# A seventh product split once more: half of a Strassen-type product of a fused attention and feed-forward kernel

## The chip, the cores and the metric

The kernel runs on one core of a Trainium2 chip. The metric is the device time of the program in microseconds, from three runs of the kernel before; one further execution was profiled. TensorE does matrix products, VectorE, ScalarE and POOL (GpSimd) do elementwise work, SP issues most of the transfers. Each engine works through its own instructions in the order in which they were written; engines wait for each other through semaphores.

## The reference

Attention between tokens and a small state in both directions, then a feed-forward layer over all rows:

```python
scores = scale * np.matmul(x, state.transpose(0, 1, 3, 2))   # x (8, 8, 512, 64), state (8, 8, 32, 64)
a = softmax(scores); xread = np.matmul(a, state)
scores2 = scale * np.matmul(state, x.transpose(0, 1, 3, 2))
a2 = softmax(scores2); sread = np.matmul(a2, x)
x = concat([xread, sread]) as (8 * 544, 512) rows
h = x @ w_in                  # 512 -> 2048
out = (h * sigmoid(h)) @ w_out   # 2048 -> 512
```

## The kernel before

The order of the work is written out by hand; the tile layer adds semaphores and buffers, and doesn't reorder. There are eight batches of 512 token rows each, and a last group of 256 state rows (8 batches of 32).

For a batch, `G1` makes the hidden values transposed: for each of 16 feature tiles `ft` two matmuls of 512 columns (L540), with weights `W1` in which the state has already been multiplied into `w_in`, and the normalised attention weights `aT` as moving data. ScalarE's SILU turns the result into `g`, bf16, 128 features by 512 tokens per `ft`. `G1` has two banks of PSUM.

The second product, `g @ w_out`, is done for batches 1 to 7 with a Strassen-Winograd scheme (`class Unit`): tokens, features and output columns are each cut in two, and seven half products take the place of eight. One half product is 256 tokens by 1024 features by 256 columns: 8 feature tiles times 2 token tiles, 16 matmuls of 256 columns (L646, `mm`). They collect in two banks of PSUM: `al` (bank o1; products 1, 6, 5) and `be` (bank o0; products 7, 2, 4, 3, each of which starts o0 anew). Sums of `g` come first: S3 is written over half of `g` (`sums3`), then S2 (`sums2`), S1 = S2 + A11 (`sums1`), S4 (`sums4`). All are VectorE additions. Sums of `w_out`, D1 to D4, are made once (`t_weights`).

One turn of the main loop (L907) handles batch `b`, and prepares batches `n = b + 1` and `m = b + 2`:

- While the G1s of `b` run (`ft` 5 to 15), units of products 1 and 7 are slipped between them (`early`, a quota per step). A unit is one feature tile, two matmuls. S3 is made in two halves at `ft` 5 and 9. At `ft` 9 VectorE also normalises the attention weights of `n` (`norm_t`: a reduction, a reciprocal, a multiplication of which POOL does half; then SP transposes the result into `aT`) and, in some batches, copies x into rows padded for the state's read (`spread_x`). In batch 7 it is the placing of the state rows' input (`place_xm`). Product 1 is copied to `kept[0]`, product 7 to `kept[1]`.
- After `ft` 15: the rest of S2; `group_a`, which is one or two pieces of `W1` of a later batch (two banks each from a ring of four, evicted half by VectorE and half by ScalarE), the transposed scores of `m`, and in batches 1, 4, 6 the state's read `sread`; then products 2, 6, 4. C11 (`block(0, 0)`) is `kept[0]` plus product 2; S1, a spread and S4 stand behind it on VectorE. Product 4 goes into o0 again, so it follows C11's sum.
- Then further pieces of `W1` (`group_b`), product 5, product 3 mixed with the first G1s of `n`, sums, stores, and on POOL the casts of the next x, `cast_x`, whose transpose `transpose_x` SP issues. The scores of the turn that follows read that transpose.

Of the kernel before, what the change touches and what calls it, by code (L numbers as in the profile page):

```python
# [8 lines left out]
FP32 = mybir.dt.float32  # L9
# [9 lines left out]
B = 8  # L19
# [4 lines left out]
DM = 512  # L24
# [18 lines left out]
def kernel(  # L43
# [23 lines left out]
    o1pool = ctx.enter_context(tc.tile_pool(name="o1pool", bufs=1))  # L67
# [21 lines left out]
    w_in_sb = pers.tile([128, 4, DF], BF16)  # L89
    w_out_sb = pers.tile([128, NFT, DM], BF16)  # L90
    wt = pers.tile([128, 4, 8, 256], BF16)
    xs = pers.tile([128, B, 128], BF16)
    xmT = pers.tile([128, 2, 4, NS, 4], BF16)
    x_rows = []
# [501 lines left out]
    def t_weights(which, k0, n, eng=nc.vector):  # L596
        k = ds(k0, n)
        for w in which:
# [6 lines left out]
            else:  # L605
                sub(eng, D4[:, k], B21[:, k], D2[:, k])

    class Unit:
        def __init__(self, b):
            self.b = b  # L610
            self.lo, self.hi = gh[b, 0], None
            self.s1 = spool.tile([128, 8, 256], BF16, tag="s1", name="s1")
            self.s2 = spool.tile([128, 8, 256], BF16, tag="s2", name="s2")
            self.al = psO.tile([128, 2, 256], FP32, tag="o1", name="o")
            self.be = None
            self.o = [
                opool.tile([128, 2, DM], FP32, tag=f"o_sb{i}", name="o_sb") for i in range(2)
            ]
# [39 lines left out]

        def sums2(self, k0, n):
            k = ds(k0, n)  # L660
            sub(nc.vector, self.s2[:, k], self.hi[:, k, 256:512], self.lo[:, k, 256:512])

        def sums1(self):
            for k0 in (0, 4):
                k = ds(k0, 4)
                add(nc.vector, self.s1[:, k], self.s2[:, k], self.lo[:, k, 0:256])

        def sums4(self):
            for k0 in (0, 4):
                k = ds(k0, 4)  # L670
                sub(nc.vector, self.hi[:, k, 0:256], self.hi[:, k, 0:256], self.s2[:, k])

        def block(self, i, c):
            return self.o[i][:, :, ds(256 * c, 256)]
# [4 lines left out]
    o_two = {}  # L679

    def store(b, tt, eng):
        if b < B:
            if tt < 2:
                o_two[tt] = opool.tile([128, 2, DM], FP32, tag=f"o_sb{tt}", name="o_sb")
            o = o_two[tt % 2][:, tt // 2]
        else:
            o = o1pool.tile([128, DM], FP32, tag="o_one", name="o_sb")
        copy(eng, o[:], outs[tt][:])
        if b < B:
            nc.sync.dma_start(out_re[ds(136 * b, 128), tt, :], o)  # L690
        else:
            nc.sync.dma_start(out_sread[ds(512, 32), ds(4 * tt, 4), :], o[:])


    def sread_out_product():
        g = gh[B, 0]
        half = lambda e, t: g[:, ds(8 * e, 8), ds(128 * t, 128)]
        a11, a21, a12, a22 = half(0, 0), half(0, 1), half(1, 0), half(1, 1)
        t8 = lambda nm: spool.tile([128, 8, 128], BF16, tag=nm, name=nm)
        s1, s2 = t8("s1"), t8("s2")  # L700
        u1, u3 = (spool.tile([128, 256], FP32, tag=nm, name=nm) for nm in ("u1", "u3"))
        o = [o1pool.tile([128, DM], FP32, tag=f"o_s{i}", name="o_s") for i in range(2)]
        al = psO.tile([128, 256], FP32, tag="o1", name="o")

        def product(left, right, to=None, first=True, c=0, n=256):
            if to is None:
                to = bank([128, 256], FP32, "o_s")
            for k in range(8):
                nc.tensor.matmul(  # L709
                    to[:, 0:n],  # L710
                    left[:, k],
                    right[:, k, ds(c, n)],
                    start=(first and k == 0),
                    stop=(k == 7),
                    skip_group_check=True,
                )
            return to

        def out(t, c, n, queue):
            queue.dma_start(  # L720
                out_sread[ds(512, 32), ds(4 * t, 4), ds(c, n)], o[t][:, ds(c, n)]
            )

        lo, hi = ds(0, 256), ds(256, 256)
        s3 = a21
        product(a11, B11, al)
        for k0, n in ((0, 6), (6, 2)):
            k = ds(k0, n)
# [6 lines left out]
        copy(nc.scalar, u1[:], al[:])  # L735
        p4 = product(a22, D4)
        add(nc.vector, u1[:], u1[:], o[1][:, hi])
        sub(nc.vector, s2[:], a12, s2[:])
        add(nc.vector, o[1][:, lo], u1[:], p4[:])
        product(s1, D1, al, False)  # L740
        copy(nc.scalar, u3[:], al[:])
        add(nc.vector, o[1][:, hi], o[1][:, hi], u3[:])
# [164 lines left out]
    for b in range(1, B):  # L907
# [1 line left out]
        m = n + 1  # L909
        u = Unit(b)  # L910
        lead = 3 if b == 1 else LEADS
        last = 6 if b < 3 else 8
        todo = [(1, k) for k in range(last)] + [(7, k) for k in range(8)]
        todo += [(1, k) for k in range(last, 8)]
        n_todo = len(todo)

        def unit():
            p, k = todo.pop(0)
            u.mm(p, k)
            if (p, k) == (1, 7):  # L920
                copy(nc.vector, u.kept[0][:], u.al[:])
            if (p, k) == (7, 7):
                copy(nc.vector, u.kept[1][:], u.be[:])

        def early(j):
            while (
                todo
                and todo[0][1] + (0 if todo[0][0] == 1 else 2) <= j - 2
                and (n_todo - len(todo)) * (NFT - lead) < 16 * (j + 1 - lead)
            ):  # L930
                unit()

        for j in range(lead, NFT):
            upto(NFT * b + j + 1)
            if j == 8:
                u.hi = gh[b, 1]
            if j == max(lead, 5):
                if b == 1:
                    t_weights((3,), 4, 4)
                    transpose_x(3)  # L940
                u.sums3(0, 4)
                if 1 < b and m + 1 < B:
                    fetch_x(m + 1)
                if b == 2:
                    for v in range(2):
                        evict_state(v, (nc.vector, nc.gpsimd)[v], 4, 4)
            if j == 9:
                u.sums3(4, 4)
                if b == 1:
                    for v in range(2):  # L950
                        evict_state(v, (nc.vector, nc.gpsimd)[v], 2, 2)
                    t_weights((2, 4), 4, 4, nc.gpsimd)
                elif n < B:
                    norm_t(n)
                    if b in SREAD_AT:
                        spread_x(n)
                else:
                    for half in range(2):
                        place_xm(half, nc.vector)
            early(j)  # L960
            if j == 13:
                u.sums2(0, 4)
# [49 lines left out]
        def units(p, leads={}):  # L1012
            nonlocal step
            for k in range(8):
                u.mm(p, k)
                if n == B and (p != 6 or k > 5):
                    upto(NFT * B + 2 + (step + 1) * (NFT - 2) // 26)
                    step += 1
                    if (p, k) == (3, 1):
                        sread_diff()  # L1020
# [6 lines left out]
        if b == 1:  # L1027
# [5 lines left out]
            fetch_x(m + 1)  # L1033
            exps_t(m)
            out_a()
        else:
# [64 lines left out]
```

## Time and profile before

| | |
|---|---|
| median of 3 runs | 203.32 us (202.95 to 205.41) |
| profiled execution | 202.72 us |
| its span, first to last instruction | 200.9 us |
| mean granted TensorE clock | 1.00 |
| matmuls of G1, 128x512 | x252, 72.7 us busy |
| matmuls of half products, 128x256 | x336, x224 and x224; 48.6, 33.0 and 27.4 us busy |
| VectorE's wait of `o_sb` for TensorE | 23.0 us in 12 waits, the longest 5.1 |
| POOL's wait of `o_sb` for ScalarE | 63.5 us in 13 waits |
| transfers | 28.71 MB, mean 143 GB/s |

Times in the profile are in microseconds from the start of the span; in a timeline row the first number is the start, the second the time from the first start to the last end of the merged instructions, `xN` how many they are. Matmuls are pipelined, so that a row's end lies beyond the start of the next one. `out<-in` names what is written and read. A kernel line can be that of a helper: L162 is any copy on VectorE or POOL, L591 and L594 are subtractions and additions, L646 is any matmul of a half product. By ft 15 of each batch the main loop has reached, in the profiled execution: batch 3 at 90.14 us, batch 4 at 111.13, batch 5 at 133.01, batch 6 at 153.12, batch 7 at 174.20.

### The profile page before, as it was taken

To read this page: it belongs to the slowest core of one execution; us is meant where nothing else is said; L and a number is where in the kernel's file an instruction comes from. 1 tells how busy PE (TensorE), PEld (TensorE's weight loads), DVE (VectorE), ACT (ScalarE), POOL (GpSimd) and SP (SyncE) were. 2 spreads that over 40 slices of the span, in tenths; PEclk is the share of its full clock that TensorE was granted. 3 is DMA by queue.
4 is the path that set the end of the run, shared out by engine and by line. 5 is a ranking of instruction groups with operands and counts; after the bars stand their busy time and mean duration, and the time that the engine had idled before them with its cause. 6 is when DMAs were issued, how large, how long until landed. Compare 5 with 4: busy or idle time off the path is not lost.

```text
span 200.9 us, 4650 instructions
## 1 busy us (share of the span) xinstructions
PE 194.4 (97%) x1912; PEld 130.5 (65%) x1912; DVE 139.3 (69%) x244; ACT 138.3 (69%) x245; POOL 72.3 (36%) x89
## 2 busy tenths in 40 slices
PE   7799999999999999999999999999999999999992
PEld 2444435467766676667766676668666876688881
DVE  2852756989997899388938974779369955872072
ACT  2885657889767887778787957888588167724530
POOL 8674333795535602730373034323202230002200
PEclk9999999999999999999999999999999999999999
DMA  5999999993056995594239912943142005000232
GB/s 193 197 206 207 256 253 353 240 233 86 5 162 181 245 267 111 209 279 90 52 151 200 230 32 55 256 102 30 37 197 55 13 3 209 0 3 0 84 128 104
DMA packets 40821, 28.71 MB, mean 143 GB/s; under 512 B 27360, under 2 KB 37472, under 8 KB 40800
## 3 DMA queue, kind: packets, MB, share of 16 engines
q1 hardware_dynamic: 34592, 20.52, 39.8%
q0 software_dynamic: 5920, 7.64, 18.3%
q8 instruction: 15, 0.25, 0.5%
q10 hardware_dynamic: 288, 0.26, 0.4%
q14 instruction: 6, 0.05, 0.1%
HBM read 17.43 MB, written 8.91 MB: 131 GB/s over the span
## 4 chain that ended last, share of the span: by engine, by line
PE 93%; DMA 4%; DVE 0%; POOL 0%; ACT 0%; issue 0%; POOLq 0%
PE o L646 43%; PE h L540 27%; PE ps_w L473 5%; DMA w_in_sb<-in_moe_w_in_dram 4%; PE h L558 4%; PE o L577 3%; PE o_a L577 3%; PE o_s L709 2%; PE o L709 1%; PE ps_sr L420 1%; PE ps_scT L336 1%; PE ps_busy L168 1%; PE h L522 1%; PE ps_xt L257 1%; PE ps_at L402 1%; PE ps_sc L310 0%
## 5 line engine op out<-in xcount | busy, mean ns | idle before, releaser
L568 ACT ACTIVATE g<-h 128x512 bf16<-128x512 f32 (+1 forms) x142 | 79.9, 573 | 34.5 <-PE h L540 23.7
L646 PEld LDWEIGHTS <-g 128*128 128x128 bf16 x560 | 54.2, 98 | 29.2 <-issue 0.5
L540 PE MATMUL h<-aT,W 128*128 128x512 bf16 x252 | 72.7, 379 | 0.2 <-ACT W L160 0.2
L646 PE MATMUL o<-w_out_sb,g 128*128 128x256 bf16 x336 | 48.6, 273 | 0.0
L646 PE MATMUL o<-wt,g 128*128 128x256 bf16 x224 | 33.0, 273 | 0.0
L594 POOL TENSOR_TENSOR o_sb<-o_sb,kept 128x512 f32<-128x512 f32 x7 | 11.0, 1568 | 54.8 <-ACT o_sb L160 39.6
L540 PEld LDWEIGHTS <-W 128*128 128x128 bf16 x252 | 24.4, 98 | 8.7 <-issue 0.9
L646 PE MATMUL o<-wt,s 128*128 128x256 bf16 x224 | 27.4, 273 | 0.0
L594 DVE TENSOR_TENSOR o_sb<-o_sb,o 128x512 f32<-128x512 f32 x14 | 9.6, 683 | 23.9 <-PE o L646 20.5
L162 DVE CAST W<-ps_w 128x512 bf16<-128x512 f32 (+1 forms) x35 | 21.8, 666 | 6.1 <-PE ps_w L473 5.9
L646 PEld LDWEIGHTS <-s 128*128 128x128 bf16 x224 | 21.5, 98 | 4.4 <-issue 2.0
L160 ACT ACTIVATE W<-ps_w 128x512 bf16<-128x512 f32 (+1 forms) x31 | 16.4, 583 | 5.3 <-PE ps_w L473 5.2
L591 DVE TENSOR_TENSOR g<-g 128x1024 bf16<-128x1024 bf16 x15 | 11.6, 775 | 9.1 <-ACT g L568 9.0
L162 POOL CAST x_nat<-x_f 128x512 bf16<-128x512 f32 x24 | 15.8, 700 | 5.4 <-issue 3.9
L594 POOL TENSOR_TENSOR o_sb<-kept,o_sb 128x512 f32<-128x512 f32 x7 | 8.9, 1268 | 23.9 <-ACT o_sb L160 23.9
L160 ACT ACTIVATE o_sb<-o 128x512 f32<-128x512 f32 x15 | 8.9, 595 | 9.8 <-issue 6.6
L591 DVE TENSOR_TENSOR g<-g,s 128x1024 bf16<-128x1024 bf16 x14 | 13.7, 1019 | 0.0
L366 POOL TENSOR_TENSOR an<-e,rcn 128x512 bf16<-128x512 bf16 x5 | 7.7, 1540 | 16.1 <-DVE rcn L364 15.6
L162 DVE COPY kept<-o 128x512 f32<-128x512 f32 x14 | 9.6, 686 | 4.2 <-PE o L646 4.1
L591 DVE TENSOR_TENSOR s<-g 128x512 bf16<-128x512 bf16 (+3 forms) x23 | 12.0, 550 | 0.1
L577 PEld LDWEIGHTS <-g 128*128 128x128 bf16 x64 | 5.8, 98 | 7.0 <-issue 0.8
L473 PE MATMUL ps_w<-w_in_sb,stT 64*32 64x512 bf16 (+1 forms) x264 | 10.2, 375 | 0.1
(106 smaller groups left out, 214.7 us busy)
## 6 DMA issues: line engine op xcount, KB each, us to landing
out_dram<-o_sb SPq DMA_DIRECT2D x14, 512.0 KB, 2.7
x_f<-in_x_dram SPq DMA_DIRECT2D x6, 512.0 KB, 4.8
x_f<-in_x_dram POOLq DMA_DIRECT2D x2, 1024.0 KB, 11.4
x_f<-in_x_dram SPq DMA_DIRECT2D x2, 1024.0 KB, 6.5
w_out_sb<-in_moe_w_out_dram POOLq DMA_DIRECT2D x6, 256.0 KB, 11.3
w_in_sb<-in_moe_w_in_dram POOLq DMA_DIRECT2D x3, 512.0 KB, 10.5
x_f<-in_x_dram POOLq DMA_DIRECT2D x2, 512.0 KB, 14.5
out_dram<-o_sb SPq DMA_DIRECT2D x4, 256.0 KB, 5.5
```

The source lines that it names most:

```text
L160: nc.scalar.activation(dst, src, func=COPY, bias=0.0)
L162: eng.tensor_copy(dst, src)
L366: eng.tensor_tensor(a[:, hg], e2[b][:, hg], rc[:, hg].to_broadcast([128, 4, 4, NS]), op=MULT)
L473: nc.tensor.matmul(pss[f, hg][ds(32 * s, 32), 0:n], stT[ds(r, 64), b, h // 2, s % 2, :], w_in_sb[ds(r, 64), h // 2, ds(f, n)], start=True, ...
L540: nc.tensor.matmul(h_ps[k][:], W1[b][:, hg, ds(128 * ft, 128)], aT[b][:, hg, :, :], start=(hg == 0), stop=(hg == 1), skip_group_check=True,)
L558: nc.tensor.matmul(ps[:, 0:256], w_in_sb[:, kt, ds(128 * ft, 128)], xmT[:, :, kt].rearrange("p t n b -> p t (n b)"), start=(kt == 0), stop ...
L568: nc.scalar.activation(gt[k], ps[:, 0:n], func=SILU, bias=0.0)
L577: nc.tensor.matmul(outs[tt][:], gt[b * NFT + ft][:, ds(128 * tt, 128)], w_out_sb[:, ft, :], start=(ft == 0), stop=(ft == NFT - 1), skip_gr ...
L591: eng.tensor_tensor(dst, a, c, op=SUB)
L594: eng.tensor_tensor(dst, a, c, op=ADD)
L646: nc.tensor.matmul(to[:, t, :], left[:, ds(128 * t, 128)], right[:, k, :], start=first and t == 0, stop=(k == 7), skip_group_check=True,)
L709: nc.tensor.matmul(to[:, 0:n], left[:, k], right[:, k, ds(c, n)], start=(first and k == 0), stop=(k == 7), skip_group_check=True,)
```

## The change

For batches 3 to 7 product 7, S3 times D3, is itself cut in two three ways and done with seven inner products of 4 matmuls of 128 columns. Inner sums of S3 (`inner_sums`) are made on VectorE at `ft` 5 and 9, and inner sums of D3 (`inner_weights`) once in batch 1. Inner products 1, 6 and 5 collect in a bank of the ring (`chain`), 2, 3, 4 and 7 in quarters of o0; VectorE puts the four quarters of `kept[1]` together after the fifth, which is the last to run. The quota of `early` spreads 15 units over one step less. `norm_t` moves from `ft` 9 of batch `n - 1` to the end of the turn before, behind product 3. `sums1` moves ahead of product 2 and C11. Spreads of x move behind S4, two of them in batch 2. Half of `place_xm` moves to POOL, and before product 2 of batch 7 there is one more G1 of the state rows. Some tiles of the tail share buffers of other tiles.

```diff
+    wt2 = pers.tile([128, 4, 4, 128], BF16)
...
+    def quarters(a):
+        return {
+            (e, c): a[:, ds(4 * e, 4), ds(128 * c, 128)] for e in range(2) for c in range(2)
+        }
+
+    def inner_weights(which, eng):
+        d = [wt2[:, i] for i in range(4)]
+        y = quarters(D3)
+        a, c = {
+            0: (y[0, 1], y[0, 0]),
+            1: (y[1, 1], d[0]),
+            2: (y[1, 1], y[0, 1]),
+            3: (y[1, 0], d[1]),
+        }[which]
+        sub(eng, d[which], a, c)
+
+    INNER = (3, 4, 5, 6, 7)
...
+        def inner_sums(self, which):
+            x = quarters(self.lo[:, :, ds(256, 256)])
+            if self.inner is None:
+                self.inner = spool.tile([128, 4, 4, 128], BF16, tag="s1", name="inner")
+            t = [self.inner[:, i] for i in range(4)]
+            for i in which:
+                if i == 1:
+                    add(nc.vector, t[0], x[0, 1], x[1, 1])
+                elif i == 2:
+                    sub(nc.vector, t[1], t[0], x[0, 0])
+                elif i == 3:
+                    sub(nc.vector, t[2], x[0, 0], x[0, 1])
+                else:
+                    sub(nc.vector, t[3], x[1, 0], t[1])
+
+        def inner_mm(self, i):
+            x, y = quarters(self.lo[:, :, ds(256, 256)]), quarters(D3)
+            t, d = self.inner, wt2
+            if self.chain is None:
+                self.chain = bank([128, 128], FP32, "o_ch")
+                self.be = psO.tile([128, 2, 256], FP32, tag="o0", name="o")
+            q = self.be.rearrange("p t (c n) -> p (t c) n", c=2)
+            ch = self.chain[:]
+            left, right, to, where = {
+                1: lambda: (x[0, 0], y[0, 0], ch, 1),
+                2: lambda: (x[1, 0], y[1, 0], q[:, 0], 0),
+                3: lambda: (t[:, 3], y[1, 1], q[:, 2], 0),
+                4: lambda: (x[1, 1], d[:, 3], q[:, 1], 0),
+                5: lambda: (t[:, 0], d[:, 0], ch, 1),
+                6: lambda: (t[:, 1], d[:, 1], ch, 1),
+                7: lambda: (t[:, 2], d[:, 2], q[:, 3], 0),
+            }[i]()
+            for k in range(4):
+                nc.tensor.matmul(to, left[:, k], right[:, k],
...
+            kept = self.kept[1]
+            if i == 1:
+                copy(nc.vector, kept[:, 0, 0:128], ch)
+            elif i == 6:
+                copy(nc.vector, kept[:, 1, 0:128], ch)
+            elif i == 5:
+                first = kept[:, :, 0:128]
+                u3 = spool.tile([128, 1, 128], FP32, tag="inner_u3", name="inner_u3")
+                copy(nc.vector, u3[:, 0], ch)
+                add(nc.vector, kept[:, :, 128:256], q[:, 2:4], u3.to_broadcast([128, 2, 128]))
+                add(nc.vector, first, first, q[:, 0:2])
+                add(nc.vector, kept[:, 1, 0:128], kept[:, 1, 0:128], q[:, 3])
...
-        last = 6 if b < 3 else 8
-        todo = [(1, k) for k in range(last)] + [(7, k) for k in range(8)]
-        todo += [(1, k) for k in range(last, 8)]
+        inner = b in INNER
+        if inner:
+            todo = [(1, k - 8, k + 2) for k in range(7)] + [(7, 1, 9), (1, -1, 9)]
+            todo += [(7, 2, 10), (7, 4, 10), (7, 7, 11), (7, 6, 12), (7, 3, 12), (7, 5, 13)]
+        else:
+            last = 6
+            todo = [(1, k - 8, k + 2) for k in range(last)]
+            todo += [(7, k - 8, k + 4) for k in range(8)]
+            todo += [(1, k - 8, k + 2) for k in range(last, 8)]
...
             while (
                 todo
-                and todo[0][1] + (0 if todo[0][0] == 1 else 2) <= j - 2
-                and (n_todo - len(todo)) * (NFT - lead) < 16 * (j + 1 - lead)
+                and todo[0][2] <= j
+                and (n_todo - len(todo)) * (NFT - lead - bool(inner)) < n_todo * (j + 1 - lead)
             ):
                 unit()
...
                 u.sums3(0, 4)
+                if inner:
+                    u.inner_sums((3,))
...
                 u.sums3(4, 4)
+                if inner:
+                    u.inner_sums((1, 2, 4))
...
-                elif n < B:
-                    norm_t(n)
-                    if b in SREAD_AT:
-                        spread_x(n)
-                else:
+                elif b == 2:
+                    norm_t(3)
+                elif n == B:
                     for half in range(2):
-                        place_xm(half, nc.vector)
+                        place_xm(half, (nc.vector, nc.gpsimd)[half])
...
         if 2 < b < B - 1:
             out_a()
+        if b > 1:
+            u.sums1()
         if n == B:
-            upto(NFT * B + 2)
+            upto(NFT * B + 3)
...
-        else:
-            u.sums1()
-            if n < B and b not in SREAD_AT:
-                spread_x(n)
...
         units(4)
         u.sums4()
+        if 1 < b < B - 2:
+            for i in {2: (3, 4)}.get(b, (b + 2,)):
+                spread_x(i)
         add(nc.vector, u.block(1, 0), u.block(1, 0), u.be[:])
...
         if b == 1:
             group_b()
+            for i in range(4):
+                inner_weights(i, (nc.vector, nc.gpsimd)[i % 2])
         units(3, {1: 2, 3: 3, 5: 4, 7: 5})
+        if 1 < b and m < B:
+            norm_t(m)
         add(nc.vector, u.block(0, 1), u.block(0, 1), u.be[:])
```

More of the change, by code (lines that the diff above doesn't have):

```diff
@@ L66 @@
     opool = ctx.enter_context(tc.tile_pool(name="opool", bufs=1))
-    o1pool = ctx.enter_context(tc.tile_pool(name="o1pool", bufs=1))
     spool = ctx.enter_context(tc.tile_pool(name="spool", bufs=1))
@@ L611, in __init__ @@
             self.lo, self.hi = gh[b, 0], None
-            self.s1 = spool.tile([128, 8, 256], BF16, tag="s1", name="s1")
-            self.s2 = spool.tile([128, 8, 256], BF16, tag="s2", name="s2")
+            self.s1 = self.s2 = None
             self.al = psO.tile([128, 2, 256], FP32, tag="o1", name="o")
             self.be = None
+            self.chain = None
+            self.inner = None
+            self.begun = set()
             self.o = [
@@ L660, in sums2 @@
             k = ds(k0, n)
+            if k0 == 0:
+                self.s2 = spool.tile([128, 8, 256], BF16, tag="s2", name="s2")
             sub(nc.vector, self.s2[:, k], self.hi[:, k, 256:512], self.lo[:, k, 256:512])
         def sums1(self):
+            self.s1 = spool.tile([128, 8, 256], BF16, tag="s1", name="s1")
             for k0 in (0, 4):
@@ new lines, in inner_mm @@
+        def inner_mm(self, i):
[16 more added lines that the diff above has]
+            for k in range(4):
+                nc.tensor.matmul(
+                    to,
+                    left[:, k],
+                    right[:, k],
+                    start=where not in self.begun,
+                    stop=(k == 3),
+                    skip_group_check=True,
+                )
+                self.begun.add(where)
+            kept = self.kept[1]
[7 more added lines that the diff above has]
+                copy(nc.vector, u3[:, 0], ch)
+                add(
+                    nc.vector,
+                    kept[:, :, 128:256],
+                    q[:, 2:4],
+                    u3.to_broadcast([128, 2, 128]),
+                )
+                add(nc.vector, first, first, q[:, 0:2])
+                add(nc.vector, kept[:, 1, 0:128], kept[:, 1, 0:128], q[:, 3])
@@ L681, in store @@
     def store(b, tt, eng):
[L682 to L685, printed above, removed]
-        else:
-            o = o1pool.tile([128, DM], FP32, tag="o_one", name="o_sb")
+        if tt < 2:
+            o_two[tt] = opool.tile([128, 2, DM], FP32, tag=f"o_sb{tt}", name="o_sb")
+        o = o_two[tt % 2][:, tt // 2]
         copy(eng, o[:], outs[tt][:])
-        if b < B:
-            nc.sync.dma_start(out_re[ds(136 * b, 128), tt, :], o)
-        else:
-            nc.sync.dma_start(out_sread[ds(512, 32), ds(4 * tt, 4), :], o[:])
+        nc.sync.dma_start(out_re[ds(136 * b, 128), tt, :], o)
     def sread_out_product():
@@ L700, in sread_out_product @@
         s1, s2 = t8("s1"), t8("s2")
-        u1, u3 = (spool.tile([128, 256], FP32, tag=nm, name=nm) for nm in ("u1", "u3"))
-        o = [o1pool.tile([128, DM], FP32, tag=f"o_s{i}", name="o_s") for i in range(2)]
+        both_u = xpool.tile([128, 4, 256], FP32, tag="x_nat", name="u")
+        u1, u3 = both_u[:, 0], both_u[:, 1]
+        o = [spool.tile([128, DM], FP32, tag=f"kept{i}", name="o_s") for i in range(2)]
         al = psO.tile([128, 256], FP32, tag="o1", name="o")
@@ L734, in sread_out_product @@
         add(nc.vector, s1[:], s2[:], a11)
-        copy(nc.scalar, u1[:], al[:])
+        copy(nc.scalar, u1, al[:])
         p4 = product(a22, D4)
-        add(nc.vector, u1[:], u1[:], o[1][:, hi])
+        add(nc.vector, u1, u1, o[1][:, hi])
         sub(nc.vector, s2[:], a12, s2[:])
-        add(nc.vector, o[1][:, lo], u1[:], p4[:])
+        add(nc.vector, o[1][:, lo], u1, p4[:])
         product(s1, D1, al, False)
-        copy(nc.scalar, u3[:], al[:])
-        add(nc.vector, o[1][:, hi], o[1][:, hi], u3[:])
+        copy(nc.scalar, u3, al[:])
+        add(nc.vector, o[1][:, hi], o[1][:, hi], u3)
         out(1, 0, 512, nc.sync)
@@ L911 @@
         lead = 3 if b == 1 else LEADS
-        last = 6 if b < 3 else 8
-        todo = [(1, k) for k in range(last)] + [(7, k) for k in range(8)]
-        todo += [(1, k) for k in range(last, 8)]
+        inner = b in INNER
[7 more added lines that the diff above has]
+            todo += [(1, k - 8, k + 2) for k in range(last, 8)]
         n_todo = len(todo)
         def unit():
[L918 to L923, printed above, removed]
+            p, k, _ = todo.pop(0)
+            if k > 0:
+                u.inner_mm(k)
+                return
+            u.mm(p, k + 8)
+            if k == -1:
+                copy(
+                    nc.vector,
+                    u.kept[int(p == 7)][:],
+                    (u.al if p == 1 else u.be)[:],
+                )
         def early(j):
@@ L952 @@
                     t_weights((2, 4), 4, 4, nc.gpsimd)
-                elif n < B:
-                    norm_t(n)
-                    if b in SREAD_AT:
-                        spread_x(n)
-                else:
+                elif b == 2:
+                    norm_t(3)
+                elif n == B:
                     for half in range(2):
-                        place_xm(half, nc.vector)
+                        place_xm(half, (nc.vector, nc.gpsimd)[half])
             early(j)
@@ L1016, in units @@
                 if n == B and (p != 6 or k > 5):
-                    upto(NFT * B + 2 + (step + 1) * (NFT - 2) // 26)
+                    upto(NFT * B + 3 + (step + 1) * (NFT - 3) // 26)
                     step += 1
@@ L1035 @@
             out_a()
-        else:
-            u.sums1()
-            if n < B and b not in SREAD_AT:
-                spread_x(n)
         if m < B:
```

## The prediction

> **What bounds the kernel now.** I read the page's busy times first, then the chain that ended last, then TensorE's waits, and then VectorE and TensorE side by side where a batch's seventh product ends.
>
> ```profile
> PE 194.4 (97%) x1912; PEld 130.5 (65%) x1912; DVE 139.3 (69%) x244; ACT 138.3 (69%) x245; POOL 72.3 (36%) x89
> ...
> PEclk9999999999999999999999999999999999999999
> ...
> PE 93%; DMA 4%; DVE 0%; POOL 0%; ACT 0%; issue 0%; POOLq 0%
> ```
>
> TensorE carries the chain (93%) at the full clock, and none of its waits after the first 10 us is longer than 0.2 us. A column removed from it is therefore worth its time, and a wait added to it costs its time: nothing later has idle time that would absorb it. What matters is whether VectorE, 69% busy on average, is late anywhere. In batch 6 (ft 15's G1 starts at 153.12) VectorE answers
>
> ```profile
> 153.97 0.69 DVE L162 COPY kept<-o 128x512 f32<-128x512 f32 x1
> 154.58 0.75 DVE L591 TENSOR_TENSOR s<-g 128x512 bf16<-128x512 bf16 x2
> 155.25 0.68 DVE L162 CAST W<-ps_w 128x512 bf16<-128x512 f32 x1
> 155.85 0.74 DVE L438 RECIPROCAL rc<-ps_sr 32x4 f32<-32x4 f32 x4
> 156.63 0.42 DVE L441 TENSOR_TENSOR xm<-ps_sr,rc 128x256 bf16<-128x256 f32 x1
> 156.97 0.68 DVE L162 CAST W<-ps_w 128x512 bf16<-128x512 f32 x1
> 157.57 0.68 DVE L594 TENSOR_TENSOR o_sb<-kept,o 128x512 f32<-128x512 f32 x1
> 158.16 1.28 DVE L594 TENSOR_TENSOR s<-s,g 128x1024 bf16<-128x1024 bf16 x2
> ```
>
> and TensorE
>
> ```profile
> 155.04 1.92 PE L646 MATMUL o<-w_out_sb,g 128*128 128x256 bf16 x16
> 156.80 1.91 PE L646 MATMUL o<-wt,s 128*128 128x256 bf16 x16
> 158.55 0.71 PE L646 MATMUL o<-wt,g 128*128 128x256 bf16 x5
> ```
>
> VectorE has no gap from 153.97 to the end of S1. The C11 sum (157.57, done 158.25) reads bank o0, which product 4 overwrites at 158.55: 0.2 us of room. So in this stretch VectorE is as late as TensorE allows.
>
> **What the matmuls give.** The half product goes from 16 matmuls of 256 columns to 7 x 4 = 28 of 128. The tail has both kinds, back to back:
>
> ```profile
> 194.25 1.04 PE L709 MATMUL o<-wt,s 128*128 128x256 bf16 x8
> ...
> 196.00 1.06 PE L709 MATMUL o_s<-w_out_sb,s 128*128 128x128 bf16 x16
> ```
>
> The last of a group takes 0.27 or 0.22, so (1.04 - 0.27)/7 = 0.11 us each for 256 columns (0.109 over sixteen) and (1.06 - 0.22)/15 = 0.056 for 128. That makes 16 x 0.109 = 1.74 against 28 x 0.056 = 1.57: 0.18 less a batch, 0.9 in five. The upper end for 128 columns is a weight load that hides behind nothing, 98 ns in the page's LDWEIGHTS groups: 28 x 0.098 = 2.74, 1.0 more a batch than now. I take 0.056: it is the same shape, with a new weight for each.
>
> The Trainium skill (TensorE: Matmul & The Clock Gate, Back-to-back issue gap) speaks against the split: it gives some 81 ns for a matmul of 128 columns in a stream of weight loads and matmuls. By that the half product would take 28 x 0.081 = 2.27, half a microsecond more than now, and the sum below would be 3.5 us higher. The row above is such a stream and contradicts it.
>
> **What VectorE gets.** (1) Four inner sums of 128x512 bf16, 0.33 each by the pair at 154.58: one behind the first half of S3, three behind the second. Normalisation and spread left that place (1.21 + 0.35 + 0.69, and 0.69 to 1.54), and TensorE needs the sums only three or four G1s later; without that cover 1.0. Nothing. (2) The last inner product now stands ahead of ft 15's G1, because the quota ends a step earlier. With T the start of that G1, its last matmul ends at T + 0.16 (0.22 - 0.056), and a copy starts 0.04 after that (in batch 3 the matmul ends at 90.95, the copy starts at 90.99). Then a copy of 128x128, two additions of 128x256 and one of 128x128 must free o0. Rows: 0.42 for 128x256 from PSUM, 0.29 for an addition of 128x128; 0.03 between dependent ones, 0.08 overlap otherwise. A copy of 128x128 isn't shown; between 0.2 and 0.42 I take 0.29. Sum 0.29 + 0.03 + 0.42 - 0.08 + 0.42 + 0.03 + 0.29 = 1.40, done T + 1.61. The wait sits on the weight load, so product 2 starts some 0.18 later, T + 1.79. (3) S1, two of 0.60, moves ahead of the C11 sum.
>
> From T, with the s2 halves after the chain (T + 1.53 to 2.20), W casts 0.60 each, and product 4 at 0.08 after C11:
>
> - Batches 3 and 5: product 2 at T + 1.79 (before: 90.14 to 91.76, 1.62). Two casts to 3.40, S1 to 4.61, C11 to 5.30, product 4 at T + 5.38; before 95.26 - 90.14 = 5.12. 0.26 late each.
> - Batch 4: product 2 waits as now for scores that follow ft 15's SILU (T + 2.51). Cast 2.80, reciprocals and product of the s read 4.11, S1 5.32, C11 6.01, product 4 at 6.09 against 6.01. 0.08 late.
> - Batch 6: casts, reciprocals and product as above to 4.52, S1 to 5.73, C11 to 6.42, product 4 at 6.50; before 158.55 - 153.12 = 5.43. 1.07 late.
> - Batch 7: no casts; C11 waits for product 2 anyway, which follows SILUs. Nothing.
>
> Up to T a batch has 8 units of 0.218 and 7 of 0.224 where it had 15 of 0.218: 0.04 later, 0.2 in five. Sum: 0.26 + 0.08 + 0.26 + 1.07 + 0.2 = 1.9 us **longer**; that is the 0.9 gained, less 2.8 of new waits. Without S1's move batch 6 would be 1.07 less, so that move is the largest single term. A POOL operation beside S1 would lengthen it (S4 took 2.36 beside one, 1.28 without): up to 1.1 more; with quicker small evictions 0.4 less a batch.
>
> **What moves.** Normalisation (2.3 on VectorE) comes before the last C21 sum, where VectorE waits for TensorE 2.2 to 2.5 us: hidden. But on POOL its multiplication now stands ahead of the four casts of x, and on SP the aT transpose ahead of the last store, the xT transpose and the x load. In batch 3 the casts started at 102.64; W casts end at 100.8, reduction and reciprocal at 102.4, POOL's 1.54 after its sum at 102.70 ends at 104.25: 1.6 later. The xT transpose, issued at 105.41 with a median of 5.0 to landing, is read at 112.10: 1.7 of room. Three batches (2, 3, 4) have this; at the longest landing, 7.0, each would wait 1.6 to 2. I take 0.1 in all. Spreads behind S4 stand ahead of the sum that frees o0 for product 3: in batch 4 1.4 of room (120.54 to 121.94) against 0.69 to 1.54, in batch 2 two spreads, about 0.7 of room after S1 has filled a wait of 0.39: 0 to 1.0 altogether, I take 0. The weights of the inner product (two operations on VectorE, two on POOL at about 1.1, half of 2.2) fall into idle 1.51 (before 61.50) and 3.90 (before 62.56). POOL takes half of place_xm where it has nothing else. Buffers that share tags are long free. All 0; on the path they would be 1 to 3 us.
>
> The profiled run of before took 202.72 (span 200.9, 1.8 around it): 202.72 + 1.9 + 0.1 = 204.7. The median of the runs is 203.32, 0.6 higher, which would give 205.3. Prediction 205.0.
>
> **Rivals.** *The gain stays* (0.24): VectorE's evictions or S1 come earlier than my rows say, and only the 0.9 is left: 202.72 - 0.9 = 201.8, on the median 202.4. For it: VectorE loses 2 to 4 us per batch ahead of T. Against it: the row at 153.97 waits for TensorE, not for VectorE's own backlog, so nothing done earlier helps. *Late xT* (0.10), on the slower side: the casts that stand behind the normalisation make scores wait in the next batch; it decides once a landing takes over 5.1. Three waits of 1.6 to 2 make 4.8 to 6 on top of 1.9: 209.5 to 210.6. For it: SP's queue gets another transpose ahead of it; against it: 3.7 is the shortest. *Weight loads show* (0.06): at 0.098 a matmul, 5 x 28 x 0.042 = 5.9 more: 210.5. *The change isn't what it says* (0.01): the order of the built program shows 28 for 16 in five batches, so hardly.
>
> **How the numbers follow.** The forecast has 0.59: its own range is 204.0 to 206.3 (product 4 waits 0.7 less in all, or the s sums and spreads meet POOL). Within 2% is about what a measurement of this kernel can tell from no change: 199.3 to 207.4. The gain and the forecast lie inside: 0.24 + 0.59, and 0.03 of mild lateness of xT; slower takes the rest of late xT, weight loads and S1 beside POOL, 0.12; faster 0.02. The range reaches down to most of the rival, 202.0, and up to 207.0, and leaves some 2 in 10 out.
>
> **What would show it.** The 28 small matmuls at about 56 ns each; three small VectorE sums ending 1.6 us after ft 15's G1 starts; product 4 named as waiting for the VectorE sum o_sb<-kept,o, some 1.1 us in batch 6 and 0.1 to 0.3 in 3, 4 and 5; product 2 waiting for the kept sums in 3 and 5; scores without a wait for xT. I am wrong if TensorE has no such waits, or if C11 ends earlier than S1 lets it, or if TensorE waits in batches 2 and 4 for o0 ahead of product 3.

## The result, and the profile after

The changed kernel takes 205.28 us (median of 22 runs, 204.33 to 207.49). The kernel before, run beside it on the same chip, takes 203.41 (22 runs, 202.56 to 205.52). The medians are 1.9 us (0.9%) apart. The ratio, which leaves out one run of after that was in a slower state, is 1.007, with a 95% interval of 1.0044 to 1.0096, or 1.4 us. So the change costs 1.4 to 1.9 us. The profiled execution took 205.22, with a span of 203.4 at a mean granted clock of 0.997; before it was 202.72, with a span of 200.9.

The page of after, at the places shown of before: busy time and share of the span, granted clock by slice, chain that ended last.

```profile
PE 194.8 (96%) x1972; PEld 130.4 (64%) x1972; DVE 154.3 (76%) x287; ACT 137.8 (68%) x245; POOL 80.2 (39%) x95
...
PEclk9999999999999999999999999999999999999998
...
PE 19%; DVE 1%; issue 0%
```

TensorE has 60 matmuls more (12 in each of five batches) and is not less busy; VectorE carries 15 us more. The chain is followed back through the last fifth of the span only (19% and 1%), so it says nothing of the batches; TensorE's waits do. Before, there was one after the first 10 us, and it was 0.2:

```profile
PE h L540 <- ACT W L160: 0.2, 1, 0.2
```

In after two are longer:

```profile
PE o L666 <- DVE o_sb L594: 1.1, 1, 1.1
PE ps_scT L336 <- DMA xT<-x_nat: 0.9, 2, 0.4
```

The first is product 4 of batch 6, the second the transposed scores in batches 4 and 5. Both are new. VectorE in batch 6, where the prediction showed before (start, time from first start to last end; ft 15's G1 starts at T = 154.51):

```profile
154.71 0.29 DVE L162 COPY inner_u<-o_ch 128x128 f32<-128x128 f32 x1
155.03 0.42 DVE L594 TENSOR_TENSOR kept<-o,inner_u 128x256 f32<-128x256 f32 x1
155.37 0.73 DVE L594 TENSOR_TENSOR kept<-kept,o 128x256 f32<-128x256 f32 x2
156.02 0.76 DVE L591 TENSOR_TENSOR s<-g 128x512 bf16<-128x512 bf16 x2
156.69 0.68 DVE L162 CAST W<-ps_w 128x512 bf16<-128x512 f32 x1
157.30 0.74 DVE L438 RECIPROCAL rc<-ps_sr 32x4 f32<-32x4 f32 x4
158.07 0.43 DVE L441 TENSOR_TENSOR xm<-ps_sr,rc 128x256 bf16<-128x256 f32 x1
158.41 0.68 DVE L162 CAST W<-ps_w 128x512 bf16<-128x512 f32 x1
159.01 1.28 DVE L594 TENSOR_TENSOR s<-s,g 128x1024 bf16<-128x1024 bf16 x2
160.21 0.68 DVE L594 TENSOR_TENSOR o_sb<-kept,o 128x512 f32<-128x512 f32 x1
```

and TensorE there, products 2, 6 and 4:

```profile
156.21 1.92 PE L666 MATMUL o<-w_out_sb,g 128*128 128x256 bf16 x16
157.97 1.91 PE L666 MATMUL o<-wt,s 128*128 128x256 bf16 x16
160.94 1.91 PE L666 MATMUL o<-wt,g 128*128 128x256 bf16 x16 [1.07 <-DVE o_sb L594]
```

S1 (159.01) now stands between the W cast and the C11 sum (160.21, done 160.89). Product 4 overwrites the bank that this sum reads, and starts 0.05 after it, at T + 6.44; before it was T + 5.43.

To see where all of the time lies, take T in each batch as the clock and read from the timelines when product 4 starts after it. T2 is the T of batch 2, T3 that of batch 3, and so on; the last column runs from T2 to the end of the span. Differences of these times are free of what happens at the start, where executions of the same code differ by several tenths:

| kernel | b3 | b4 | b5 | b6 | T2 to end |
|---|---|---|---|---|---|
| before | 5.12 | 6.01 | 5.12 | 5.43 | 131.70 |
| after | 5.32 | 6.11 | 5.44 | 6.44 | 133.73 |
| difference | 0.20 | 0.10 | 0.32 | 1.01 | 2.03 |

The four product 4s make 1.63 of the 2.03. From product 4 to the next T is 0.03 to 0.06 longer in each of batches 3 to 6, 0.16 in all; from batch 7's T to the end it is 0.02. From T2 to T3 it is 0.22 longer, 0.18 of it where the scores of batch 2 start later, 0.04 after xT lands. The other 0.45 of the two spans lies ahead of T2, and isn't put down to the change: two of the kernels below whose code is the same up to there (called both and best) have T2 at 69.20 and 70.04.

### The profile page after: what moved, and what is told of

The parts are those of the page before. It is cut to its first block, busy times and chain, and to the rows that moved or that the text cites. A ratio compares the mean times of both kernels' runs of the same rounds, so it can differ in the third digit from the quotient of the medians.

```text
span 203.4 us, 4815 instructions
## 1 busy us (share of the span) xinstructions
PE 194.8 (96%) x1972; PEld 130.4 (64%) x1972; DVE 154.3 (76%) x287; ACT 137.8 (68%) x245; POOL 80.2 (39%) x95
## 5 line engine op out<-in xcount | busy, mean ns | idle before, releaser
L666 PEld LDWEIGHTS <-g 128*128 128x128 bf16 x480 | 46.4, 98 | 24.7 <-issue 1.7
L666 PE MATMUL o<-w_out_sb,g 128*128 128x256 bf16 x336 | 49.3, 273 | 0.2 <-DVE kept L162 0.2
L540 PEld LDWEIGHTS <-W 128*128 128x128 bf16 x252 | 23.4, 98 | 8.2 <-issue 0.9
L666 PE MATMUL o<-wt,g 128*128 128x256 bf16 x144 | 19.3, 273 | 1.1 <-DVE o_sb L594 1.1
L162 POOL CAST x_nat<-x_f 128x512 bf16<-128x512 f32 x24 | 18.5, 809 | 1.5 <-DMA x_f<-in_x_dram 1.5
L591 DVE TENSOR_TENSOR g<-g 128x1024 bf16<-128x1024 bf16 x15 | 12.5, 834 | 3.9 <-ACT g L568 3.8
L591 DVE TENSOR_TENSOR s<-g 128x512 bf16<-128x512 bf16 (+3 forms) x23 | 11.1, 510 | 0.1
L577 PEld LDWEIGHTS <-g 128*128 128x128 bf16 x64 | 5.8, 98 | 7.0 <-issue 0.8
L591 DVE TENSOR_TENSOR g<-g,s 128x1024 bf16<-128x1024 bf16 x14 | 10.2, 772 | 0.0
L577 PE MATMUL o_a<-w_out_sb,g 128*128 128x512 bf16 x32 | 10.0, 379 | 0.0
L594 DVE TENSOR_TENSOR s<-s,g 128x1024 bf16<-128x1024 bf16 x15 | 9.7, 684 | 0.0
```

The lines of the kernel that those rows point to most:

```text
L162: eng.tensor_copy(dst, src)
L540: nc.tensor.matmul(h_ps[k][:], W1[b][:, hg, ds(128 * ft, 128)], aT[b][:, hg, :, :], start=(hg == 0), stop=(hg == 1), skip_group_check=True,)
L577: nc.tensor.matmul(outs[tt][:], gt[b * NFT + ft][:, ds(128 * tt, 128)], w_out_sb[:, ft, :], start=(ft == 0), stop=(ft == NFT - 1), skip_gr ...
L591: eng.tensor_tensor(dst, a, c, op=SUB)
L594: eng.tensor_tensor(dst, a, c, op=ADD)
L666: nc.tensor.matmul(to[:, t, :], left[:, ds(128 * t, 128)], right[:, k, :], start=first and t == 0, stop=(k == 7), skip_group_check=True,)
```

## The experiments

All ten compute the whole of the reference. Times are medians; the ratio is to the kernel before, run on the same chip in the same series, and it is the one to compare where two kernels are of different series.

**S1 back behind product 6 and C11.**

```diff
-        if b > 1:
-            u.sums1()
         if n == B:
             upto(NFT * B + 3)
...
             out_a()
+        else:
+            u.sums1()
```

> S1 goes back behind C11's sum, to its old place after product 6; all else as changed. Theory (S1 ahead of C11 makes product 4 wait in batch 6): the wait of 1.1 there and the 0.16 in batch 3 go, C11 in batch 6 is done before TensorE reaches product 4, and the median is 1.2 to 1.4 lower than the changed kernel, 203.9 to 204.1. Rival (the longer chain of evictions of the seventh product is what makes C11 late, wherever S1 stands): product 4 of batch 6 still waits 0.8 or more, median 204.8 to 205.3.

203.87 us (12 runs), ratio 1.0027 (1.0002 to 1.0052). C11 is first again, S1 after it:

```profile
158.88 0.68 DVE L594 TENSOR_TENSOR o_sb<-kept,o 128x512 f32<-128x512 f32 x1
159.48 1.29 DVE L594 TENSOR_TENSOR s<-s,g 128x1024 bf16<-128x1024 bf16 x2
```

Product 4 of batch 6 starts at T + 5.24, 1.20 sooner: two additions of 0.60. From T2 to the end it is 132.23, 1.50 less than after. The place of S1 is the largest part of the loss. Scores still wait for xT, 0.4 us in one batch.

**S1 behind C11 in batch 6 alone.**

```diff
-        if b > 1:
+        if b > 1 and b != 6:
             u.sums1()
...
+        elif b == 6:
+            u.sums1()
```

> The changed kernel with S1 behind C11 in batch 6 alone. Theory (the wait of batch 6 is the one large cost of S1's place): 1.1 to 1.25 lower than the changed kernel, 204.0 to 204.2; from batch 6's last G1 to batch 7's 21.0 where the changed kernel took 22.15, and the other batches as in the changed kernel. Rival (the waits of the other batches count as much): 204.6 to 205.0.

204.01 us (12 runs), ratio 1.0035 (1.001 to 1.0059). One batch carries most of what S1's place costs: the ratio falls from 1.007 to 1.0035, where moving S1 in all batches gave 1.0027 (the intervals overlap), and from T6 to T7 both kernels take 20.96, where after took 22.15. In batches 3 and 5 S1's place costs 0.16 each: product 4 starts at T + 5.32 in the next run, where xT is in time and S1 ahead of C11, and at T + 5.16 in the run after that, where S1 is behind.

**Casts of x ahead of POOL's half of the normalisation, and the xT transpose ahead of that of aT.**

```diff
         if 1 < b and m < B:
-            norm_t(m)
+            rest = norm_t(m, m + 1 < B)
...
             transpose_x(m + 1)
+            if b > 1:
+                rest()
```

(`rest` is POOL's multiplication and the aT transpose; VectorE's part stays.)

> At the end of a turn POOL's half of the normalisation and the aT transpose go behind the casts of x and the xT transpose; VectorE's part stays. Theory (xT lands late because its casts stand behind the normalisation): the two waits of the transposed scores for xT, 0.44 idle each, go; part returns in their place, because product 2 then waits for the kept sums in batch 5 and product 4 for C11 in batches 4 and 5; median 0.5 to 0.9 below the changed kernel, 204.4 to 204.8. Rival (the transpose is late by SP's other transfers): the waits stay, median 205.3.

205.51 us (6 runs, 204.31 to 207.21), ratio 1.0105 (1.0052 to 1.0158). The gain of 0.5 to 0.9 that was expected didn't come: the time can't be told from that of after. The trace says why a gain is small. No scores wait for xT, but product 4 starts at 5.32, 6.03, 5.32 and 6.44 after T, and in batch 6 still waits for C11:

```profile
162.95 1.25 PE L680 MATMUL o<-wt,g 128*128 128x256 bf16 x10 [1.07 <-DVE o_sb L608]
```

In batches 4 and 5 only 0.08 and 0.12 come back for 0.9 of waiting removed: the scores' second half then waits for ScalarE's last SILU, and product 4 of batch 5 for S1. T2 to end is 133.37, 0.36 less than after, but half of that lies between T2 and T3, which the edit doesn't reach: it starts with the transpose at the end of turn 2, which batch 3 reads. From T3 on it is 0.19. Waits that stand one behind the other don't add.

**Both of these repairs together.** The edits above, S1 in all batches.

> Both edits together. Theory: the split's 0.9 isn't earned even then, because product 2 stands behind the evictions and the last SILU with no unit between: 203.1 to 203.5, about the kernel before. Rival (with these two waits gone nothing hides the shorter TensorE work): 202.4 to 202.7, 0.4% under the kernel before.

203.27 us (12 runs), ratio 0.9986 (0.9965 to 1.0006): back at the kernel before, with the split in it. T2 to end is 132.23, against 131.70 before, and 0.45 of the difference lie between T2 and T3, nearly all of it where the scores of batch 2 wait for xT in this execution. From T3 to the end it is 110.90 against 110.81. So both losses are named, and the question is where the 0.9 us of saved matmul time is.

**The moves without the split.**

```diff
-    INNER = (3, 4, 5, 6, 7)
+    INNER = ()
```

> No batch has its seventh product split (16 matmuls of 256 columns again, one copy to kept[1], no inner sums); every move stays. Theory (the moves lose the time, the split itself gains some): product 4 waits about 1.0 in batch 6 and 0.2 in 3 and 5, xT about 0.4 twice; 205.2 to 205.9. Rival (the split's small operations lose it, the moves are free): 203.2 to 203.6.

204.82 us (11 runs), ratio 1.0072 (1.0041 to 1.0102): by the ratio as slow as with the split. Product 4 starts at 5.26, 6.02, 5.26 and 6.38, so late by 0.14, 0.01, 0.14 and 0.95. The moves alone lose most of the time: T2 to end is 133.06, 1.36 more than before, where the whole change takes 2.03 more. It is somewhat faster than expected, as xT is late in one batch only, by 0.3.

**The repaired moves without the split.** The kernel with both repairs, and `INNER = ()`.

> As 'both', without the split (16 matmuls of 256 columns again, one copy). Theory: the moves without S1's and with the casts ahead cost nothing: 203.2 to 203.6, within 0.1% of 'both', so that the split by itself gives nothing there. Rival (the split in 'both' does give 0.9, and the remaining moves take it): 204.0 to 204.4.

203.52 us (12 runs), ratio 1.0024 (0.9998 to 1.005). The trace has product 4 at 5.12, 6.01, 5.12 and 5.43 as before. From T3 to the end it takes 110.88, against 110.90 with the split: in the two profiled executions the split gives nothing in that form. (The medians are of two series; their ratios to the kernel before, 1.0024 and 0.9986, have intervals that overlap by little, and would leave it some 0.8.) The rows of TensorE behind ft 15 of batch 3 show it, first with the split:

```profile
90.54 0.59 PE L554 MATMUL h<-aT,W 128*128 128x512 bf16 x2
91.07 0.62 PE L487 MATMUL ps_w<-w_in_sb,stT 64*32 64x512 bf16 x16
91.51 0.72 PE L336 MATMUL ps_scT<-xT,stT 64*32 64x512 bf16 x8
92.20 0.61 PE L680 MATMUL o<-w_out_sb,g 128*128 128x256 bf16 x4
```

and without:

```profile
90.68 0.60 PE L554 MATMUL h<-aT,W 128*128 128x512 bf16 x2
91.12 0.38 PE L680 MATMUL o<-w_out_sb,g 128*128 128x256 bf16 x2
91.43 0.63 PE L487 MATMUL ps_w<-w_in_sb,stT 64*32 64x512 bf16 x16
91.87 0.50 PE L336 MATMUL ps_scT<-xT,stT 64*32 64x512 bf16 x8
92.30 0.50 PE L680 MATMUL o<-w_out_sb,g 128*128 128x256 bf16 x3
```

Without the split, a unit of the half products stands behind ft 15 and the scores take 0.50. With it, that unit is ahead of ft 15, and the scores take 0.72: their second half follows ScalarE's SILU of ft 15, the second of the two SILUs (ft 14 and 15) in this row, which ends at 91.77

```profile
90.52 1.25 ACT L582 ACTIVATE g<-h 128x512 bf16<-128x512 f32 x2 [0.28 <-PE h L554]
```

Product 2 starts at T + 1.66 with the split and at T + 1.62 without, though there is a unit less between. What comes off the matmuls before T is lost again behind it.

**Evictions earlier, and one unit left behind ft 15.** Both repairs, and:

```diff
-            elif i == 5:
+            elif i == 3:
                 first = kept[:, :, 0:128]
+                add(nc.vector, first, first, q[:, 0:2])
+                add(nc.vector, kept[:, 1, 0:128], kept[:, 1, 0:128], q[:, 3])
+            elif i == 5:
...
-                add(nc.vector, first, first, q[:, 0:2])
-                add(nc.vector, kept[:, 1, 0:128], kept[:, 1, 0:128], q[:, 3])
...
-            todo = [(1, k - 8, k + 2) for k in range(7)] + [(7, 1, 9), (1, -1, 9)]
-            todo += [(7, 2, 10), (7, 4, 10), (7, 7, 11), (7, 6, 12), (7, 3, 12), (7, 5, 13)]
+            todo = [(1, k - 8, k + 2) for k in range(7)] + [(7, 1, 9)]
+            todo += [(7, 2, 10), (7, 4, 10), (7, 7, 11), (7, 6, 12), (7, 3, 12), (7, 5, 13), (1, -1, 15)]
...
-                and (n_todo - len(todo)) * (NFT - lead - bool(inner)) < n_todo * (j + 1 - lead)
+                and (n_todo - len(todo)) * (NFT - lead) < n_todo * (j + 1 - lead)
...
+            if j == 13 and inner:
+                u.sums2(0, 4)
             early(j)
-            if j == 13:
+            if j == 13 and not inner:
                 u.sums2(0, 4)
```

> The two edits of 'both', and the end of the seventh product rearranged: of its four last VectorE operations the two that need only inner products 1 to 4, 6 and 7 run ahead of inner product 5's copy, S2's first half runs before the step's units, and the last unit of product 1 is left to stand behind ft 15's G1, as a unit did in the kernel before. Theory (what kept the split's gain from showing is the eviction chain and the SILU after the last G1 with no unit between): bank o0 is free 0.9 after ft 15's G1 starts, product 2 starts 1.6 after it as before, and each batch keeps its 0.18: 202.4 to 202.7, ratio 0.995 to 0.997. Rival (128-column matmuls between G1s aren't worth their 56 ns each): 203.1 to 203.5.

202.51 us (12 runs, 201.96 to 203.53) against 203.17 before (29 runs): ratio 0.9968 (0.9944 to 0.9991), 0.3% faster than the kernel before, and faster than after. Behind ft 15 of batch 3, TensorE has its unit again, and the scores take 0.50:

```profile
90.90 0.59 PE L554 MATMUL h<-aT,W 128*128 128x512 bf16 x2
91.33 0.38 PE L680 MATMUL o<-w_out_sb,g 128*128 128x256 bf16 x2
...
92.09 0.50 PE L336 MATMUL ps_scT<-xT,stT 64*32 64x512 bf16 x8
```

Product 4 stands at the places of before, and from T3 to T4 it is 20.81 where before had 20.99: the 0.18 a batch. T2 to end is 131.45, 0.25 less than before. Most of the rest of the gain is lost in three small gaps on the inner products' way (0.17 in batch 5, 0.23 and 0.05 in batch 7) and in one of 0.16 at an early G1 of batch 3. That G1 starts at 80.46, 0.05 after VectorE's cast of its weights, and the cast stands behind the two spreads of batch 2. Against the repaired moves without the split, run in the same series, the split is now worth 1.0 us in the medians and 0.5 in the traces.

**The same without the unit behind ft 15.**

```diff
-            todo = [(1, k - 8, k + 2) for k in range(7)] + [(7, 1, 9)]
-            todo += [(7, 2, 10), (7, 4, 10), (7, 7, 11), (7, 6, 12), (7, 3, 12), (7, 5, 13), (1, -1, 15)]
+            todo = [(1, k - 8, k + 2) for k in range(7)] + [(7, 1, 9), (1, -1, 9)]
+            todo += [(7, 2, 10), (7, 4, 10), (7, 7, 11), (7, 6, 12), (7, 3, 12), (7, 5, 13)]
...
-                and (n_todo - len(todo)) * (NFT - lead) < n_todo * (j + 1 - lead)
+                and (n_todo - len(todo)) * (NFT - lead - bool(inner)) < n_todo * (j + 1 - lead)
```

> As 'best', but product 1's last unit stays where the change put it, so that ft 15's G1 is followed by no unit. Theory: product 2 then waits in batches 3 and 5 for the scores, whose second bank ft 15's SILU frees 1.28 after its G1 starts; 0.1 to 0.3 of the gain is left: 203.0 to 203.3. Rival (the chain of evictions alone held the gain): 202.4 to 202.7, the same as 'best'.

203.96 us (12 runs), ratio 1.004 (1.0019 to 1.0061): worse than expected. The place of one unit decides 1.45 us between this kernel and the one above it in the medians, and 1.03 from T2 to the end. Product 2 starts at T + 1.62 in batches 3 and 5 of both kernels, with the unit before it or not, and from product 4 to the next T it takes 0.22, the time of a unit, longer here. TensorE's waits show a part of it: the scores wait for the last SILU once more, and in batch 7 an inner product waits for the copy that frees its bank:

```profile
PE o_ch L743 <- DVE kept L162: 0.5, 1, 0.5
PE ps_scT L336 <- ACT g L582: 0.2, 1, 0.2
```

So earlier evictions alone don't help: the wait behind ft 15 isn't for them.

**place_xm earlier in batch 7**, on top of the best kernel, to take away its gaps there.

```diff
                     u.inner_sums((3,))
+                if n == B:
+                    for half in range(2):
+                        place_xm(half, (nc.vector, nc.gpsimd)[half])
```

(and taken out at ft 9)

> As 'best', with the state rows' input placed at ft 5 of batch 7 and not at ft 9. Theory (there VectorE's four copies stand ahead of the small evictions and delay inner products 6 and 5 by 0.2 to 0.3): batch 6's last G1 to batch 7's takes 20.8 to 20.9 in place of 21.19, the median 0.2 to 0.4 under 'best': 202.1 to 202.3. Rival (the step is long for another reason): no difference, 202.5.

202.69 us (12 runs), ratio 0.9958 (0.9934 to 0.9982). That can't be told from the best kernel, and T6 to T7 takes 21.13, not 20.8 to 20.9: the rival is nearer. The two gaps ahead of inner products 6 and 5 are gone from the trace, and one of 0.19 is at inner product 2 instead.

**The split alone.** Kernel before, with the split and none of the moves: normalisation and spreads at ft 9, S1 behind C11, place_xm on VectorE.

```diff
-                elif b == 2:
-                    norm_t(3)
-                elif n == B:
+                elif n < B:
+                    norm_t(n)
+                    if b in SREAD_AT:
+                        spread_x(n)
+                else:
...
-        if 1 < b and m < B:
-            norm_t(m)
```

(against after; S1, the spreads and place_xm as before, too)

> The kernel before with the split alone: normalisation and spreads at ft 9, S1 behind C11, all of place_xm on VectorE, two state-row G1s ahead of product 2. Theory (VectorE's queue at ft 9 is full): the copy of inner product 1 stands behind normalisation, and in batches 4 and 6 a spread as well, so that inner product 6 waits about 0.9 in batches 3 and 5, 2.4 in 4 and 6 and 1.5 in batch 7: 209 to 212. Rival (these steps are hidden there as they were before): 202.5 to 203.5.

211.71 us (4 runs, 210.45 to 213.26), ratio 1.0422 (1.0376 to 1.0469). VectorE in batch 4:

```profile
109.35 1.21 DVE L363 TENSOR_REDUCE rs<-e 128x32 f32<-128x1024 bf16 x1
110.60 0.35 DVE L364 RECIPROCAL rcn<-rs 128x32 f32<-128x32 f32 x1
110.99 0.69 DVE L366 TENSOR_TENSOR an<-e,rcn 128x512 bf16<-128x512 bf16 x1
111.60 1.54 DVE L162 COPY x_rows<-x_nat 128x2048 bf16<-128x2048 bf16 x1
113.06 0.28 DVE L162 COPY kept<-o_ch 128x128 f32<-128x128 f32 x1
```

and TensorE, which waits for that copy to use the bank again:

```profile
113.39 0.38 PE L729 MATMUL o_ch<-wt,inner 128*128 128x128 bf16 x4 [2.11 <-DVE kept L162]
...
113.83 0.98 PE L540 MATMUL h<-aT,W 128*128 128x512 bf16 x2
114.61 0.64 PE L729 MATMUL o_ch<-wt,inner 128*128 128x128 bf16 x4
```

There are five such waits, 7.0 us in all. The chain of small evictions stands behind the normalisation (batches 3 to 6) and the spread (4 and 6) on VectorE, and in batch 7 behind the copies of place_xm (1.4). So the moves of those three are what the split needs; S1's move is not, since none of these waits is for it.

## Why the prediction was right, and where not

205.0 was forecast and 205.28 measured, and the forecast's mechanism carries the largest term: S1 in batch 6. That the sum for product 4 comes out to 0.04 (1.67 forecast, 1.63 measured) is in part luck, since in batches 4 and 5 another wait stands where S1's was put. By its steps:

**Matmuls.** 56 ns for 128 columns is right. Four of them and the next instruction are 0.22 apart, here ahead of ft 15 of batch 3 in after:

```profile
90.59 0.39 PE L729 MATMUL o_ch<-wt,inner 128*128 128x128 bf16 x4
90.81 0.38 PE L540 MATMUL h<-aT,W 128*128 128x512 bf16 x1
```

Each has a new weight. The 81 ns of the Trainium skill (TensorE: Matmul & The Clock Gate, Back-to-back issue gap) would be 0.32; the measurement decides. The rival of weight loads that show falls.

**Inner sums hidden.** Right in cost. In size not: they take 0.4 to 0.7 each in batch 3 and not 0.33, but TensorE comes for them later.

**The evictions.** Forecast to end at T + 1.61; in batch 3 of after they end at T + 1.60 (copy 0.29, additions 0.42 and 0.73). Product 2 was put 0.18 after that, at T + 1.79, and starts at T + 1.66, 0.06 after them. It stands behind scores that wait for the last SILU, and loses only 0.04 to the evictions.

**Product 4.** Forecast late by 0.26, 0.08, 0.26 and 1.07 in batches 3 to 6; measured 0.20, 0.10, 0.32 and 1.01. In 3 and 6 the cause is S1 and the evictions, as said. In 4 and 5 it is not: there product 2 is late already (T + 2.60 and T + 1.94 against 2.51 and 1.62), because scores wait for xT, and product 4 follows it at the 3.50 that products 2 and 6 take. In the casts-first run, without that wait, S1 and the evictions make it 0.02 and 0.20 there.

**Up to T.** Forecast 0.04 a batch, measured 0.03 to 0.06.

**xT.** This is the step that failed: 1.6 us later, 1.7 of room, 0.1 in all. Measured: 0.44 of waiting in batch 4, 0.44 in batch 5, and some 0.2 in batch 2. TensorE in batch 4 of after:

```profile
112.56 0.41 PE L473 MATMUL ps_w<-w_in_sb,stT 64*32 64x512 bf16 x8
113.40 0.41 PE L336 MATMUL ps_scT<-xT,stT 64*32 64x512 bf16 x8 [0.44 <-DMA xT<-x_nat]
```

POOL and SP at the end of batch 3, before:

```profile
102.64 2.74 POOL L162 CAST x_nat<-x_f 128x512 bf16<-128x512 f32 x4
...
105.41 1.56 SPq L147 DMA_TRANSPOSE xT<-x_nat  x1
```

and after:

```profile
103.52 1.49 POOL L366 TENSOR_TENSOR an<-e,rcn 128x512 bf16<-128x512 bf16 x1
104.97 3.39 POOL L162 CAST x_nat<-x_f 128x512 bf16<-128x512 f32 x4
...
108.38 2.98 SPq L147 DMA_TRANSPOSE xT<-x_nat  x1
```

The transpose is issued 3.0 later and not 1.6, of which 0.9 is that batch 3's whole timeline lies later. So it is 2.1 later against its own batch: the casts start 1.4 later, and take 3.39 for 2.74. It lands after 4.98, less than the 5.1 from which lateness was said to decide. So it was the issue that was late and not the landing. The prediction took the casts' own time as fixed. VectorE shows why it isn't:

```profile
104.85 0.71 DVE L591 TENSOR_TENSOR g<-g 128x1024 bf16<-128x1024 bf16 x1
105.60 0.71 DVE L591 TENSOR_TENSOR inner<-g 128x512 bf16<-128x512 bf16 x1
107.19 0.70 DVE L591 TENSOR_TENSOR g<-g 128x1024 bf16<-128x1024 bf16 x1 [0.87 <-ACT g L568]
```

These are the halves of S3 and an inner sum. Taken singly, POOL's four casts start at 104.97, 105.98, 106.73 and 107.29, and take 1.07, 0.80, 0.61 and 1.07: the three long ones start while one of these sums is running, and end some 0.47 after it does. It is so in all traces: behind the first 50 us the twelve kernels have 192 such casts. 86 start while such an operation of VectorE runs (TENSOR_TENSOR on bf16: S3, an inner sum or the multiplication of the normalisation), and 85 of these take 0.80 to 1.08; the other 107 take 0.61 to 0.70. So a cast that meets such a sum is held up, and the split adds inner sums to meet. What the two share isn't shown.

On the time the term came out small all the same, about 0.19 from T3 to the end by the casts-first run, since in batches 4 and 5 most of it takes the place of waits for the last SILU and for S1. Batch 2's wait has another cause, which the prediction put at 0: the casts at the end of turn 1 stand behind two sums of D3 (`inner_weights`) on POOL, 2.50 us, and the transpose is issued 3.5 ahead of T2 where it was 4.0. Some executions wait for it there (0.18 in that of after, 0.41 in that with both repairs), most do not. The rival of late xT, 4.8 to 6 on top, was far too high: the transposes came 0.2 to 0.5 late and not 1.6 to 2, and it added waits that lie behind one another.

**Normalisation, spreads, buffers at 0.** In after no wait of TensorE names them, and the split-alone run shows what normalisation, spreads and place_xm would cost where they stood: 7.0 us of waits. The spreads behind S4 aren't quite free: in five of the other runs, that of the best kernel among them, an early G1 of batch 3 starts 0.16 late behind the two of batch 2.

**The gain stays** as a rival asked whether evictions and S1 could come earlier. The run with both repairs answers: with S1 out of the way and xT in time, product 4 starts at 5.16, 6.01, 5.16 and 5.24 after T, no more than 0.04 later than before, and the kernel is at 203.27, not at the rival's 202.4. So "the 0.9 gained, less 2.8 of new waits" is right as a sum and not as an account: with these waits gone, the 0.9 isn't there. With the fifth inner product ahead of ft 15 nothing is left to fill the SILU's time; the rival overlooked that. The forecast took it in without naming it, since it counted from T to product 4, where the unit behind ft 15 is gone. Only with one unit put back behind ft 15 does a part of it show.

What stays open: through what VectorE's sums hold up POOL's casts, as no run moved them alone, and why the best kernel's medians show more of the split (1.0) than its trace does (0.5). Nor was it tried to close the last gaps of the best kernel.

## What to carry to other kernels

Work taken off the busiest engine counts only if the next thing it does isn't already tied to another engine: keep a piece of independent work behind the instruction whose result everyone waits for, and judge a split by where its last piece stands. An operation moved ahead in an in-order queue can cost its whole duration to one behind it (S1: 1.20 in batch 6, 0.16 in batches 3 and 5); look for the one among those that frees a bank. When a wait stands behind another wait in the same stage, remove both before you judge either.

## What the chip showed that was not expected

In the split-alone run TensorE waits about 2.1 us in batch 4 and as long in batch 6. After the first, its clock is down for a while; after the second, it isn't. Windows of that run (time, busy time and instructions of PE, PEld, DVE, ACT and POOL, then granted clock, DMA share, GB/s):

```profile
110.40:113.90 3.50, 1.39 (x17) 0.93 (x15) 3.43 (x7) 1.19 (x2) 1.55 (x1) 1.00 1.02 269
113.90:117.30 3.40, 3.40 (x26) 1.00 (x23) 2.78 (x10) 1.74 (x3) 0.00 (x0) 0.50 0.91 160
...
160.00:164.00 4.00, 4.00 (x109) 2.74 (x107) 3.92 (x12) 2.17 (x4) 0.00 (x0) 1.00 0.34 66
```

At 0.50 over 3.4 us, at most 1.7 us are lost beside the wait itself. From T3 to T5 this run takes 4.4 us more than before, and the two waits there make 3.1 from start to start, so that some 1.3 is left for the clock (both are estimates); the rows of batch 4 above show it, 0.64 for four small matmuls that take 0.39 elsewhere. The Trainium skill (TensorE: Matmul & The Clock Gate, Part 1) gives some 3.4 us without work, in windows that run freely, until the clock goes down. Here a wait of 2.1 us was enough once in two times, with TensorE busy for 1.39 of the 3.50 us before the clock fell, and waits of 0.7 to 1.4 us in batches 3, 5 and 7 of the same run were not. The length agrees: the clock is down from 113.90 to 117.31, 3.41 us, and its two other changes in this run, at 4.67 and 209.47, lie 32 and 27 times 3.41 from these. If windows of that length follow one another all the time, the first wait (111.28 to 113.39) lies whole inside one, and the second (157.70 to 159.81) is cut at 158.27. That fits, with one case of each, and isn't more than that.
